# Unit 1's loads on GpSimd's queue, first-layer weights in three pieces, and landing delays in the planner

## The chip, the cores and the metric

The kernel runs on one core of a Trainium2 chip. The metric is device time in microseconds of one execution, lower is better. Engines are named as in the profile: PE (TensorE's matmuls; PEld its weight loads), DVE (VectorE), ACT (ScalarE), POOL (GpSimd) and SP (SyncE, which here only issues transfers).

## The reference

A gated linear recurrence is followed by a two-layer network with a squared ReLU. Per batch and head, a 48x48 state is decayed by alpha, receives the outer product of k and v, and is read by q; the outputs of the eight heads of a token, side by side, are the network's 384 inputs.

```python
batch, n_heads, seq, head_dim = (4, 8, 768, 48)
for t in range(S):
    state = alpha[:, :, t, :, None] * state + np.einsum('bhd,bhe->bhde', k[:, :, t], v[:, :, t])
    y[:, :, t] = np.einsum('bhd,bhde->bhe', q[:, :, t], state)
...
n_tokens, d_model, d_ff = (3072, 384, 2048)
h = x @ w_in
r = np.maximum(h, 0.0)
g = r * r
return (g @ w_out).astype(np.float32)
```

## The kernel before

The 3072 tokens are cut into twelve units of 256 tokens: unit g holds tokens of batch g % 4, and units 0 to 3 are the first third of each sequence. Each unit goes through a front (decays from alpha's logarithms, scaled keys and queries, transposes), scores with a causal mask, a state update, an output, then the first dense layer (eight groups of six matmuls, s1, each for two of the sixteen 128-column tiles of the hidden layer), ReLU and square, and the second dense layer (s2: two halves of the tokens, each in four parts of four matmuls over the hidden tiles).

Nothing is emitted in the order in which it is written. Every step is handed to `add` with its engine (or several to choose from), an estimated cost, a priority and what it reads and writes. `Program.schedule` then plays a list scheduler on those costs, in which transfers are modelled as three queues (SP, ACT, Pool) that share the bandwidth. It fixes each engine's order; `place` works out which semaphores each step must wait for, and `emit` writes the instructions. An engine works through its list strictly in order. Two tables correct the plan by hand: MOVED adds to a step's priority (larger is later) and CHOSEN fixes a step's engine. `fill` puts matmuls of zeros on the PE (line 1103) where the plan has it idle before the first s1 step.

The order of transfers is set by the queue that a transfer is issued on, by its priority there, and by AFTER, which makes an issue wait until another transfer has landed. `load(g)` issues alpha, k, q and v of a unit (384 KB each, tile raw, line 524). In the kernel before, SP issues the loads of all units but 2, and Pool those of unit 2 (POOL_LOADS) and the weights. `weight(lay, w)` issues each layer's weights in WS = 2 halves (tiles win and wout, line 495), read as float32 and written as bfloat16. AFTER reads there:

```python
AFTER = {(1, "v"): (0, "q"), ("win", 0): (1, "a"), ("win", 1): (1, "a"), 2: ("win", 0), ("wout", 0): ("win", 1),
         ("wout", 1): (2, "k"), 3: ("wout", 0)}
```

so both halves of the first layer wait for unit 1's alpha, unit 2's loads for the first half, the second layer's first half for the second half of the first layer, and unit 3's loads for the second layer's first half.

Lines that the prediction names: 524 a load's issue, 495 a weight's issue, 540 the logarithm of unit 0's alpha (ACT), 569 the cast of unit 0's v, 775 the state update, 904 scores, 915 the masks, 836 and 843 the output of the early units, 950 and 962 the transposes of a unit's activations and their copy to the tile xt, 1008 s1, 1016 and 1018 ReLU, 1026 and 1030 the square (sq, into the tile gt), 1049 s2, 879 the state's product with a decay (sbd).

Of the kernel before, what the change touches and what calls it, by code (L numbers as in the profile page):

```python
# [33 lines left out]
class Program:  # L34
# [9 lines left out]
    DMA_LAST = 800  # L44
    SWITCH = 95
# [67 lines left out]
    def schedule(self):  # L113
# [237 lines left out]
def bass_gla_recurrent__then__act_relu_squared_kernel(  # L351
# [13 lines left out]
    T = 256  # L365
    NST = S // T
    KT = DM // 128
# [12 lines left out]
    WS = 2  # L380
# [99 lines left out]
    FS = FT // WS  # L480

    def hidden(fj):

        w, e = divmod(fj, FS)
        return slice(w * FS * 128 + e, (w + 1) * FS * 128, FS)

    def weight(lay, w):
        cut = slice(w * FS * 128, (w + 1) * FS * 128) if lay == 0 else slice(w * FS, (w + 1) * FS)
        if lay == 0:
            src, dst = moe_w_in.rearrange("(kk p) n -> p kk n", p=128)[:, :, cut], WIN[:, :, cut]  # L490
        else:
            src = moe_w_out[w * FS * 128:(w + 1) * FS * 128, :].rearrange("(p e) n -> p (e n)", e=FS)
            dst = WOUT[:, cut, :].rearrange("p e n -> p (e n)")
        key = ("win", "wout")[lay]
        load_op[key, w] = add("pool", lambda e: e.dma_start(dst, src), 930, W_PRIO[lay] + w, writes=[(key, w)], name=f"{key}{w}",
                              dma=f"{key}{w}", lag=8600 / WS,
                              after=[load_op[AFTER[key, w]]] if (key, w) in AFTER else [])
# [3 lines left out]
    def hd(ap):  # L501
        return ap.rearrange("p (h d) -> p h d", h=H)

    def named(x):
        return next(o for o in pr.ops if o.name == x)
# [3 lines left out]
    def load(g):  # L509
        b, i = units[g]  # L510
        t0 = i * T
        p0 = g * P
        r, la, qs, kt, pm, vb, x2 = (g % n for n in (NRAW, 2, NQKS, NKQT, NPM, NV, 2))
        first, last = i == 0, i == NST - 1
        sr, sw = 2 * b + i % 2, 2 * b + (i + 1) % 2

        for j, t, nm in ((0, alpha, "a"), (1, k, "k"), (2, q, "q"), (3, v, "v")):
            src = t[b, :, t0:t0 + T, :].rearrange("h (p j) d -> p h (j d)", j=2)
            dst, key = RAW[r][:, j], ("raw", r, j)
            ring, cost, gate = "sp", 600, AFTER.get((g, nm), AFTER.get(g))  # L520
# [3 lines left out]
            load_op[g, nm] = add(ring, lambda e, dst=dst, src=src: e.dma_start(dst, src), cost, (L_PRIO[g] + j if ring == "sp" else W_PRIO[2] + 10 * g + j),  # L524
                writes=[key], name=f"ld{nm}{g}", dma=f"{nm}{r}{ring}", lag=1230,
                after=([load_op[gate]] if gate else []) + ([named(f"{BEHIND[nm]}{g - 1}")] if g >= 5 else []))
# [441 lines left out]
    def last_tile(gt, rows, p0):  # L968

        for h, cut in enumerate((slice(0, LAST_CUT), slice(LAST_CUT, DM))):  # L970
# [3 lines left out]
            def s2(pe, psS=psS, cut=cut):  # L974
# [5 lines left out]
                + [("wout", w) for w in range(WS)], writes=[keyS], name=f"s2_{G - 1}_1_{h}")  # L980
# [6 lines left out]
    def first_layer(g):  # L987
# [5 lines left out]
        for u in range(nb):  # L993
# [19 lines left out]
            add("pe", s1, pe_ns(KT * per, T), pu, reads=[("xt", s)] + sorted({("win", f // FS) for f in fjs}),  # L1013
# [18 lines left out]
    def second_layer(g):  # L1032
# [4 lines left out]
        for j in range(2):  # L1037
# [6 lines left out]
            for sg in range(4):  # L1044
                ps_ = p0 + P * 0.5 + 600 + (j * 4 + sg) * P * 0.5 / 8

                def s2(pe, sg=sg, j=j, psS=psS):
# [6 lines left out]
                    reads=[("gt", gt, fj) for fj in range(sg * FT // 4, (sg + 1) * FT // 4)] + [("wout", sg * WS // 4)],  # L1054
# [15 lines left out]
    W_PRIO = (-5e5, -4e5, -4.5e5)  # L1070
# [6 lines left out]
    AFTER.update({g: (g - 1, "q") for g in range(4, G)})  # L1077
    load(0)
    load(1)
    for w in range(WS):  # L1080
        weight(0, w)
    load(2)
    for w in range(WS):
        weight(1, w)
# [50 lines left out]
```

## Time and profile before

| | before |
|---|---|
| median of 3 runs | 176.35 us (176.1 to 176.62) |
| the profiled execution | 176.55 us, of which its span is 174.8 us |
| granted TensorE clock | 1.00 of full speed |
| PE busy | 168.1 us, 96% of the span, filler of 9.5 us included |
| DVE, ACT, POOL busy | 123.6, 113.9, 20.6 us |
| read from and written to HBM | 25.17 MB, 4.72 MB |
| transfers | 191 GB/s as a mean; Pool's queue 4.72 MB, SP's 28.32 MB |

Times in the views count from the span's start. A row of the timeline gives start, duration, engine, line, operation, output <- input, and in brackets the engine's idle time before it and what ended it. A row of a table by stretches gives the stretch, its length, busy time and number of instructions of each engine asked for, the granted clock, the share of the 16 DMA engines' time that packets took (over 1 when packets overlap in an engine) and GB/s. A row of issues gives the issuing queue, size and the time from issue to landing.

### The profile page before, as it was taken

Reading aid. Unit: us, or ns where it says so; the run is one execution under the profiler, and the core shown is the slowest. Engines: PE = TensorE matmul, PEld = TensorE weight load, DVE = VectorE, ACT = ScalarE, POOL = GpSimd, SP = SyncE. Lnnn points to the kernel's source line nnn. Section 1 sums busy time; section 2 is a strip of 40 time slices with the busy share of each in tenths; the row PEclk is TensorE's granted clock in tenths of the full one; section 3 lists DMA queues with packets and bytes.
Section 4 is the critical chain, followed back from the end, with each engine's and each line's share of the span. In section 5 each row is a group of like instructions: output and inputs, shape, how many; then the busy total and the mean of one; then the engine's idle time right before and its main releaser. Section 6 shows DMA issues by size and latency. Waiting matters only on the chain.

```text
span 174.8 us, 5089 instructions
## 1 busy us (share of the span) xinstructions
PE 168.1 (96%) x2233; PEld 130.7 (75%) x2235; DVE 123.6 (71%) x201; ACT 113.9 (65%) x205; POOL 20.6 (12%) x30
## 2 busy tenths in 40 slices
PE   7989799999999999999999999999999999999994
PEld 2655689765788588878778778788678797788773
DVE  5499597989879889988958858859659726322230
ACT  3745479637778677858688669588568564566440
POOL 3141561020402302100100100000000000000000
DMA  5999899999999899798997998899599691040022
GB/s 138 323 296 197 160 334 217 219 274 257 301 210 204 210 252 181 203 222 173 280 188 213 240 196 226 208 209 256 132 182 250 140 196 24 0 135 4 9 81 90
DMA packets 74742, 33.36 MB, mean 191 GB/s; under 512 B 71648, under 2 KB 71904, under 8 KB 74720
## 3 DMA queue, kind: packets, MB, share of 16 engines
q1 hardware_dynamic: 73184, 28.32, 70.8%
q0 software_dynamic: 1536, 4.72, 12.4%
q8 instruction: 17, 0.28, 0.6%
q14 instruction: 5, 0.04, 0.1%
HBM read 25.17 MB, written 4.72 MB: 171 GB/s over the span
## 4 chain that ended last, share of the span: by engine, by line
PE 78%; DMA 14%; ACT 3%; SPq 2%; issue 1%; DVE 0%
PE psWH L1008 33%; PE psO L1049 30%; DMA win<-in_moe_w_in_dram 5%; DMA raw<-in_alpha_dram 5%; DMA raw<-in_q_dram 3%; SPq L524 2%; PE psX L807 2%; PE psX L904 2%; PE psZ L775 2%; PE psWH L1049 2%; PE psX L976 2%; PE psX L796 1%; PE psZ L904 1%; ACT rr L1016 1%; PE psWH L648 1%; PE psO L1008 1%
## 5 line engine op out<-in xcount | busy, mean ns | idle before, releaser
L1008 PE MATMUL psWH<-xt,win 128*128 128x256 bf16 x552 | 70.8, 274 | 1.3 <-DMA win<-in_moe_w_in_dram 0.9
L1008 PEld LDWEIGHTS psWH<-xt,win 128*128 128x128 bf16 x552 | 62.8, 145 | 6.0 <-ACT rr L1016 1.2
L1049 PE MATMUL psO<-wout,gt 128*128 128x384 bf16 x352 | 66.5, 326 | 0.2 <-ACT osb L1056 0.2
L1016 ACT ACTIVATE rr<-psWH 128x512 bf16<-128x512 f32 x78 | 46.1, 595 | 21.2 <-PE psWH L1008 20.0
L1049 PEld LDWEIGHTS psO<-wout,gt 128*128 128x128 bf16 x352 | 33.0, 98 | 18.1 <-ACT osb L1056 0.4
L1026 DVE TENSOR_TENSOR gt<-rr 128x1024 bf16<-128x1024 bf16 (+1 forms) x45 | 27.2, 607 | 22.4 <-ACT rr L1016 22.0
L915 DVE TENSOR_TENSOR pm<-psX,caus 128x1024 bf16<-128x1024 f32 x12 | 14.6, 1219 | 0.9 <-PE psZ L904 0.9
L915 DVE TENSOR_TENSOR pm<-psZ,caus 128x1024 bf16<-128x1024 f32 x12 | 14.6, 1216 | 0.9 <-PE psZ L904 0.9
L1056 ACT ACTIVATE osb<-psO 128x384 f32<-128x384 f32 x18 | 8.8, 490 | 8.5 <-PE psO L1049 8.2
L1030 ACT ACTIVATE gt<-rr 128x1024 bf16<-128x1024 bf16 (+1 forms) x15 | 12.8, 857 | 1.8 <-DVE rr L1018 1.4
L710 DVE TENSOR_TENSOR qks<-raw,eq 128x384 bf16<-128x384 f32 x18 | 9.4, 554 | 4.1 <-DMA raw<-in_q_dram 3.9
L935 ACT ACTIVATE xbf<-psX 128x768 bf16<-128x768 f32 x10 | 8.1, 809 | 4.7 <-PE psX L796 4.4
L1018 DVE TENSOR_SCALAR rr<-psWH 128x512 bf16<-128x512 f32 x14 | 9.6, 686 | 1.9 <-PE psWH L1008 1.7
L1103 PE MATMUL psO<-zero 128*128 128x512 bf16 (+1 forms) x33 | 9.5, 422 | 1.4 <-DVE zero L445 1.3
L715 DVE TENSOR_TENSOR qks<-raw,ek 128x768 bf16<-128x768 f32 x11 | 10.7, 975 | 0.0
L706 ACT ACTIVATE vbf<-raw 128x768 bf16<-128x768 f32 x7 | 5.9, 839 | 4.1 <-DMA raw<-in_v_dram 4.1
L681 ACT ACTIVATE la<-raw 128x384 f32<-128x384 f32 x8 | 4.2, 521 | 4.8 <-DMA raw<-in_alpha_dram 4.7
L1103 PEld LDWEIGHTS psO<-zero 128*128 128x128 bf16 x35 | 3.5, 109 | 4.9 <-issue 1.9
L705 POOL CAST vbf<-raw 128x768 bf16<-128x768 f32 x4 | 3.5, 869 | 30.1 <-DMA raw<-in_v_dram 30.1
L870 DVE TENSOR_TENSOR smd<-psZ,sbd 128x384 bf16<-128x384 f32 x8 | 4.4, 555 | 3.6 <-PE psX L796 3.6
L640 ACT ACTIVATE lab<-prd 128x384 bf16<-128x384 f32 x10 | 5.2, 519 | 2.6 <-POOL prd L639 1.8
L879 POOL TENSOR_TENSOR sbd<-tmp,acm 128x384 bf16<-128x384 f32 x5 | 5.2, 1037 | 13.7 <-DVE tmp L877 13.7
(129 smaller groups left out, 180.7 us busy)
## 6 DMA issues: line engine op xcount, KB each, us to landing
raw<-in_alpha_dram SPq DMA_DIRECT2D x11, 384.0 KB, 3.8
raw<-in_k_dram SPq DMA_DIRECT2D x11, 384.0 KB, 4.8
raw<-in_q_dram SPq DMA_DIRECT2D x11, 384.0 KB, 4.2
raw<-in_v_dram SPq DMA_DIRECT2D x11, 384.0 KB, 4.9
out_dram<-osb SPq DMA_DIRECT2D x11, 384.0 KB, 4.0
win<-in_moe_w_in_dram POOLq DMA_DIRECT2D x2, 768.0 KB, 11.0
wout<-in_moe_w_out_dram POOLq DMA_DIRECT2D x2, 768.0 KB, 8.8
raw<-in_alpha_dram POOLq DMA_DIRECT2D x1, 384.0 KB, 4.6
```

Of the source, the lines that this page charges most:

```text
L710: add("dve", lambda e, j=j, dst=dst: e.tensor_tensor(dst, RAW[r][:, 2, :, j, :].rearrange("p (n x) d -> p n x d", x=2), EQ[la][:, j].rearr ...
L715: add("dve", lambda e, a=a, E=E: e.tensor_tensor(QKS[qs][:, a, :, :, 0:D], RAW[r][:, 1 + a].rearrange("p h j d -> p j h d"), E[la][:].rear ...
L915: add("dve", lambda e, hf=hf, psT=psT: e.tensor_tensor(PM[pm][:, hf].rearrange("p r n j t -> p (r n) (j t)"), psT[:, :, :].rearrange("p r ...
L935: add("act", lambda e: e.activation(XBF[x2][:], psX[:, :, 0:HD], AF.Copy), act_ns(2 * HD), p0 + 6100, reads=[("ps", "X", 0), ("ps", "X", 1 ...
L1008: ins = pe.matmul(psF[:, i * T:(i + 1) * T], WIN[:, kk, hidden(fj)], mov, start=(kk == 0), stop=(kk == KT - 1))
L1016: add("act", lambda e, psF=psF, rr=rr: e.activation(rr, psF, AF.Relu), act_ns(512), pu + 600, reads=[keyF], writes=[("rr", rb, half)], nam ...
L1018: alts={"dve": (lambda e, psF=psF, rr=rr: e.tensor_scalar(rr, psF, 0.0, None, ALU.max), dve_ns(512))})
L1026: add("dve", lambda e, dst=dst, sq=sq: e.tensor_tensor(dst, sq, sq, ALU.mult), 148 + k * 267, pu + 1200, reads=[("rr", rb, h) for h in ran ...
L1030: "act": (lambda e, dst=dst, sq=sq: e.activation(dst, sq, AF.Square), act_ns(k * 512))})
L1049: ins = pe.matmul(psS, GT[gt][:, fj, j, :], WOUT[:, fj, :], start=(fj == 0), stop=(fj == FT - 1))
L1056: add("act", lambda e, j=j, psS=psS: e.activation(OSB[ob][:, j], psS, AF.Copy), act_ns(DM), ps_ + 700, reads=[keyS], writes=[("osb", ob, j ...
L1103: pr.fill(lambda n: lambda pe: pe.matmul(psO[:, 0:n], ZERO[:, 0:128], ZERO[:, 0:n], skip_group_check=True), ((512, 216, 420), (256, 109, 2 ...
```

## The change

Unit 1's four loads leave SP's queue and go to Pool's, where one list, QUEUE, now sets the order: unit 1's loads, the first layer in three pieces of 4, 4 and 8 tiles (CUT), unit 2's loads, and the second layer in two. AFTER is rewritten: unit 1's alpha and k, and the first piece, wait for unit 0's alpha; its q and v, and the second piece, for unit 0's k; the third piece for unit 0's q; unit 2's loads for the second piece; the second layer's first half for the third piece and its second half for unit 2's k; unit 3's loads, as before, for the second layer's first half. The hidden layer's columns are dealt to tiles within a piece (`hidden`), and the second layer's rows are loaded to match. The planner's model of a transfer gets a delay by name (LATE), and MOVED and CHOSEN are new lists.

```diff
+    LATE = {"ld0": 300, "ld1": 450, "ld2": 800, "win0": 1000, "win1": 600, "win2": 600, "wout0": 800, "wout1": 500}
...
     MOVED = {
-       "s2_2_1_3": 7106, "y2": 20605, "vc2": 1344, "sq3_1": 11423, "re2_7": -11717, "re1_6": 4811, "sq3_5": -1032,
...
+       "s2_2_1_3": 39407, "s2_2_0_2": 34013, "s2_2_0_0": -42665, "lb5": 16519, "s1_2_6": 19412, "m1i5": -22795,
+        "s2_1_1_1": 168415, "sq0_7": 73172, "s2_2_1_2": 37834, "s1_0_5": 52602, "s2_0_1_3": 98172,
...
     CHOSEN = {
-       "re1_6": "dve", "et1_2": "act", "sq2_3": "act", "bk4": "pool", "xv3": "act", "re3_2": "dve", "sq3_5": "dve",
+       "et10_0": "dve", "vc1": "pool", "et0_1": "act", "sq0_7": "act", "sd1": "pool", "re1_1": "dve", "sq1_5": "act",
+        "et1_2": "act", "oe0_1": "act", "sa3": "dve", "sq2_1": "pool", "sq2_3": "act", "re2_5": "dve",
+        "sq2_6": "act", "sq2_7": "pool", "sd4": "pool", "re3_3": "act", "sq3_3": "dve", "re3_5": "dve",
+        "sq3_6": "pool", "sq3_7": "pool", "sq4_1": "dve", "pr6": "pool", "vc6": "pool",
     }
...
-                    land(op, t + self.DMA_LAST)
+                    unit = "ld" + op.name[3:] if op.name.startswith("ld") else op.name
+                    land(op, t + self.DMA_LAST + self.LATE.get(unit, 0))
...
-    POOL_LOADS = {2: "akqv"}
+    CUT = (4, 4, 8)
+    QUEUE = "a1 k1 q1 v1 win0 win1 win2 a2 k2 q2 v2 wout0 wout1".split()
...
+    def piece(fj):
+
+        w, w0 = 0, 0
+        while fj >= w0 + CUT[w]:
+            w, w0 = w + 1, w0 + CUT[w]
+        return w, w0, CUT[w]
...
-        w, e = divmod(fj, FS)
-        return slice(w * FS * 128 + e, (w + 1) * FS * 128, FS)
...
+        w, w0, n = piece(fj)
+        return slice(w0 * 128 + fj - w0, (w0 + n) * 128, n)
...
+    def weight(name):
+        key, w = name[:-1], int(name[-1])
+        if key == "win":
+            w0, n = sum(CUT[:w]), CUT[w]
+            cut = slice(w0 * 128, (w0 + n) * 128)
             src, dst = moe_w_in.rearrange("(kk p) n -> p kk n", p=128)[:, :, cut], WIN[:, :, cut]
         else:
...
+            w0, n, e = 8 * w, 8, piece(8 * w)[2]
+            src = moe_w_out[w0 * 128:(w0 + n) * 128, :].rearrange("(s p e) n -> p s (e n)", p=128, e=e)
+            dst = WOUT[:, w0:w0 + n, :].rearrange("p (s e) n -> p s (e n)", e=e)
+        load_op[name] = add("pool", lambda e: e.dma_start(dst, src), 930, -6e5 + QUEUE.index(name), writes=[(key, w)], name=name,
+                            dma=name, lag=8600 * n / 16, after=gate(name))
...
-            if nm in POOL_LOADS.get(g, ""):
-                ring, cost = "pool", 930
...
+            if name in QUEUE:
+                ring, cost, at = "pool", 930, -6e5 + QUEUE.index(name)
...
-    AFTER = {(1, "v"): (0, "q"), ("win", 0): (1, "a"), ("win", 1): (1, "a"), 2: ("win", 0), ("wout", 0): ("win", 1),
-             ("wout", 1): (2, "k"), 3: ("wout", 0)}
+    AFTER = {"win0": "a0", "a1": "a0", "k1": "a0", "q1": "k0", "v1": "k0", "win1": "k0", "win2": "q0", "a2": "win1", "k2": "win1",
+             "q2": "win1", "v2": "win1", "wout0": "win2", "wout1": "k2", 3: "wout0"}
```

More of the change, by code (lines that the diff above doesn't have):

```diff
@@ L376, in bass_gla_recurrent__then__act_relu_squared_kernel @@
     DENSE = {0: 19172, 1: 35978, 2: 46351, 3: 61182, 11: 160500}
-    POOL_LOADS = {2: "akqv"}
+    CUT = (4, 4, 8)
+    QUEUE = "a1 k1 q1 v1 win0 win1 win2 a2 k2 q2 v2 wout0 wout1".split()
     RATIO = 4
     NRAW, NQKS, NKQT, NPM, NV, NXT, NGT, NRR, NOSB = 4, 3, 3, 2, 4, 4, 2, 4, 2
-    WS = 2
     LATE_STATE = (1, 2)
@@ L502, in hd, with gate @@
         return ap.rearrange("p (h d) -> p h d", h=H)
+    def gate(*names):
+        return [load_op[AFTER[x]] for x in names if x in AFTER][:1]
     def named(x):
@@ L979, in last_tile @@
             add("pe", s2, pe_ns(FT, n), p0 + h, reads=[("gt", gt, fj) for fj in range(FT)]
-                + [("wout", w) for w in range(WS)], writes=[keyS], name=f"s2_{G - 1}_1_{h}")
+                + [("wout", w) for w in range(2)], writes=[keyS], name=f"s2_{G - 1}_1_{h}")
             add("act", lambda e, psS=psS, cut=cut: e.activation(OSL[:, cut], psS, AF.Copy), act_ns(n), p0 + 700 + h,
@@ L1012, in first_layer @@
             fjs = range(u * per, (u + 1) * per)
-            add("pe", s1, pe_ns(KT * per, T), pu, reads=[("xt", s)] + sorted({("win", f // FS) for f in fjs}),
+            add("pe", s1, pe_ns(KT * per, T), pu, reads=[("xt", s)] + sorted({("win", piece(f)[0]) for f in fjs}),
                 writes=[keyF], name=f"s1_{g}_{u}")
@@ L1053, in second_layer @@
                 add("pe", s2, pe_ns(FT // 4, DM), ps_,
-                    reads=[("gt", gt, fj) for fj in range(sg * FT // 4, (sg + 1) * FT // 4)] + [("wout", sg * WS // 4)],
+                    reads=[("gt", gt, fj) for fj in range(sg * FT // 4, (sg + 1) * FT // 4)] + [("wout", sg // 2)],
                     writes=[keyS], name=f"s2_{g}_{j}_{sg}")
@@ L1069, in bass_gla_recurrent__then__act_relu_squared_kernel @@
     L_PRIO[0], L_PRIO[1] = -9e5, -8e5
-    W_PRIO = (-5e5, -4e5, -4.5e5)
     ORDER = ["f0", "k0", "p0", "f1", "y0", "p1", "k1", "y1", "f2", "p2", "k2", "s0", "s1"]
@@ L1074, in bass_gla_recurrent__then__act_relu_squared_kernel @@
     ORDER += [f"y{G - 1}"]
-    AFTER = {(1, "v"): (0, "q"), ("win", 0): (1, "a"), ("win", 1): (1, "a"), 2: ("win", 0), ("wout", 0): ("win", 1),
-             ("wout", 1): (2, "k"), 3: ("wout", 0)}
-    AFTER.update({g: (g - 1, "q") for g in range(4, G)})
+    AFTER = {"win0": "a0", "a1": "a0", "k1": "a0", "q1": "k0", "v1": "k0", "win1": "k0", "win2": "q0", "a2": "win1", "k2": "win1",
+             "q2": "win1", "v2": "win1", "wout0": "win2", "wout1": "k2", 3: "wout0"}
+    AFTER.update({g: f"q{g - 1}" for g in range(4, G)})
     load(0)
[L1079 to L1084, printed above, removed]
+    early = []
+    for x in QUEUE:
+        if x[0] == "w":
+            weight(x)
+        elif int(x[1:]) not in early:
+            early.append(int(x[1:]))
+            load(early[-1])
+    for g in (1, 2):
+        if g not in early:
+            load(g)
     for st in ORDER:
```

19 lines of the change are left out of this document (5 added, 14 removed), and 7 rows, old and new, of the table MOVED.

## The prediction, made before the changed kernel ran

> **What bounds the kernel now.** I read the shares of the page first, then the busy time of TensorE in stretches that I cut where its work changes, then the chain of waits, and last the timeline and the DMA queues of the first 37 us.
>
> The page's first line, and TensorE alone by stretch (length, busy time and instructions, granted clock, DMA share, GB/s):
>
> ```profile
> PE 168.1 (96%) x2233; PEld 130.7 (75%) x2235; DVE 123.6 (71%) x201; ACT 113.9 (65%) x205; POOL 20.6 (12%) x30
> ...
> 16.78:19.03 2.25, 1.39 (x37) 1.00 1.14 214
> 19.03:23.50 4.47, 4.23 (x80) 1.00 0.82 213
> 23.50:32.20 8.70, 8.70 (x93) 1.00 1.04 247
> 32.20:37.00 4.80, 4.35 (x65) 1.00 1.05 261
> 37.00:172.55 135.55, 134.69 (x1788) 1.00 0.81 179
> ```
>
> From 19.03 us on, TensorE stands still for only 0.24 + 0.00 + 0.45 + 0.86 = 1.55 us, at full clock. No edit to loads can shorten that stretch by more; what is left to win lies ahead of 19.03, where the first dense group (six matmuls of line 1008) begins. What holds it back is in the chain and the timeline:
>
> ```profile
> 9.42 9.56 DMA win<-in_moe_w_in_dram
> 19.03 0.87 PE psWH L1008 x6
> ...
> 16.22 0.56 DVE L962 COPY xt<-psX 128x768 bf16<-128x768 bf16 x1
> 17.53 0.42 PE L904 MATMUL psX<-kqt 64*64 64x128 bf16 x16
> 17.77 0.39 PE L904 MATMUL psZ<-kqt 64*64 64x128 bf16 x16
> ```
>
> Unit 0's activations are ready at 16.22 + 0.56 = 16.78 us. Until 19.03 TensorE has only unit 1's scores (17.53 to 18.16, 0.63 us) and filler, and waits for the first half of the first-layer weights. So 2.25 - 0.63 = 1.62 us are lost there. With the 1.55 us above, 3.17 us is all that can be had while xt0 is ready at 16.78: a floor of 176.55 - 3.17 = 173.4 us against the profiled execution (176.55 us, of which 174.8 is span). That execution is 0.2 us above the median of the runs, 176.35.
>
> **What the first landing costs the rest.** The weights go through one queue, and they are limited by transfer:
>
> ```profile
> L495 POOL DMA_DIRECT2D win<-in_moe_w_in_dram x2: 788/860/932, 9.4 to 10.4; - x2
> DMA to landing us min/median/max: 9.6/11.0/12.4
> ...
> q1 hardware_dynamic: 864, 0.33, 117.5%
> ...
> q0 software_dynamic: 723, 1.44, 108.4%
> ...
> 23.51 0.88 PE L1008 MATMUL psO<-xt,win 128*128 128x256 bf16 x6
> 19.03:23.50 4.47, 3.06 (x24) 2.59 (x24) 1.00 0.82 213
> ```
>
> The first two lines are the tile win: issues at 9.4 and 10.4, landings at 9.4 + 9.6 = 19.0 and 10.4 + 12.4 = 22.8 us. The two queue lines are the transfers of 9 to 10 us (SP's loads) and of 12.7 to 20 us (Pool's weights): packets, MB, share of 16 engines' time. The engines are full in both, so landings go by the bytes queued ahead. A packet of a load takes 1.175 x 16 / 864 = 21.8 ns for 384 bytes, one of the weights 1.084 x 7.3 x 16 / 723 = 175 ns for 2 KB in SBUF (4 KB of float32 read). The last line is line 1008 alone: 24 matmuls, four of unit 0's eight groups, are done by 23.50. The fifth, the first to need the second half, starts at 23.51, 0.7 us after that half landed.
>
> **The change, part by part.**
>
> *Unit 1's loads to Pool.* SP loses four issues, and Pool gains four. Unit 1's alpha and k now wait for unit 0's alpha, q and v for unit 0's k.
>
> ```profile
> 4.35 0.94 ACT L540 ACTIVATE laf<-raw 128x384 bf16<-128x384 f32 x2 [0.96 <-DMA raw<-in_alpha_dram]
> 3.09 1.15 SPq L524 DMA_DIRECT2D raw<-in_v_dram  x1
> raw<-in_v_dram SPq DMA_DIRECT2D x1, 384.0 KB, 4.8
> 19.27 0.95 POOL L524 DMA_DIRECT2D raw<-in_alpha_dram  x1 [5.71 <-DMA win<-in_moe_w_in_dram]
> 20.21 0.89 POOL L524 DMA_DIRECT2D raw<-in_k_dram  x1
> 7.97 0.82 POOL L569 CAST vbf<-raw 128x768 bf16<-128x768 f32 x1 [5.03 <-DMA raw<-in_v_dram]
> 13.89 0.36 PE L836 MATMUL psX<-smd,kqt 128*64 128x96 bf16 x8
> ```
>
> Unit 0's alpha has landed by 4.35, its v lands at 3.09 + 4.8 = 7.9. Pool then issues at 4.3, 5.3, 6.2 and 7.1 (0.95 and 0.89 us each), and the three first-layer pieces at about 8.0, 8.8 and 9.7 by the 0.86 us above, done at 10.5. SP's queue works until 7.9, and two Pool loads are issued by then. So the DMA engines find work without a gap, and unit 1's loads pass as they did. Cost: nothing, covered by unit 0's transfers; without that cover it would be Pool's lead from issue to first byte, under 2 us (19.27 to where the queue is full again at 21.0, below). What queues behind these issues on Pool is unit 0's v cast (7.97 before): it goes to ACT or waits until 10.5, done by 11.4. Unit 0's output reads it at 13.89. Cost 0, at most 0.5.
>
> *Pieces of 4, 4 and 8 tiles.* The first piece is half as long. Ahead of it lie eight loads, and the weights' data began right behind the last of these before too. It should land about 393 KB earlier at the 1.44 MB in 7.3 us above: 2.0 us before 19.0, at 17.0; if some engines lag, as the late landings suggest, 16 to 17.5. Unit 0's first two groups thus start at about 17.0, its next two need the second piece near 19.0. Half-size packets: a line through 21.8 ns for 384 bytes and 175 ns for 4 KB gives 90 ns for 2 KB, so two cost 181 where one cost 175. For 384 packets' worth on 16 engines that is 24 x 6 ns, about 0.15 us later for the last piece. If a packet cost 175 ns whatever its size, it would be 24 x 175 ns = 4.2 us. The loads' small packets show time going with bytes, so I take 0.15 and keep a little of the other end in the range.
>
> So the last piece lands at 22.8 + 0.15 = 22.9 or 23.0. This limits the gain: groups five to eight still wait for it. By then TensorE has done four groups, unit 1's scores, state and output. Before, it was there at 23.51, so 0.55 us are won, and 0.35 more if unit 1's x-transposes (0.34 us at 25.04) are done by then too, since unit 1's output no longer stands behind late groups:
>
> ```profile
> 19.36 1.21 DVE L915 TENSOR_TENSOR pm<-psX,caus 128x1024 bf16<-128x1024 f32 x1
> 22.78 0.29 PE psX L836 x8
> 25.04 0.34 PE psX L950 x6
> ```
>
> Unit 1's last mask ends at 20.57 and its output ran at 22.78; it may run near 21.2, and its transposes, 2.3 us behind it before with two groups between, near 23.
>
> *Unit 2's loads and the second layer.* They wait for the second piece instead of the first half, the second layer's first half for the last piece.
>
> ```profile
> 23.00 0.56 POOL L495 DMA_DIRECT2D wout<-in_moe_w_out_dram  x1
> wout<-in_moe_w_out_dram POOLq DMA_DIRECT2D x1, 768.0 KB, 7.8
> 32.20 1.46 PE L1049 MATMUL psO<-wout,gt 128*128 128x384 bf16 x8
> ...
> q0 software_dynamic: 9, 0.02, 28.6%
> ```
>
> The second layer's first half landed at 30.8, and was first used at 32.20. The last line is 20.4 to 21.0 us: the engines ran nearly empty there, since unit 2's loads were issued at 19.27. Issued behind the second piece, while the last is still moving, they close that gap, 0.4 us, which pays for the 0.15. So weights needed at 32.2 - 0.9 = 31.3 are there by about 30.6, and this wait is hidden by 0.7 us. If that cover went, the gain would.
>
> *The planner.* Due times and engine choices of some 40 steps change. They add no work for TensorE. A better order may recover a part of the 0.45 us of 32.20 to 37.00; I take 0.2 (bounds: plus 1.55, and a loss that the second rival prices).
>
> Sum: 0.55 + 0.35 + 0.2 = 1.1 us. 176.55 - 1.1 = 175.45 against the profiled execution, 175.25 against the median: 175.3. The forecast's own range is 0.6 to 2.0 us of gain, 174.4 to 175.8, because the last piece may land up to a microsecond sooner (a single late engine may have set 22.8).
>
> **The rivals.**
>
> *Nothing comes of it.* The last piece is no earlier than the second half was, so groups start earlier and TensorE waits longer before the fifth. For this: the engines are full from 9 to 20 us and no byte is removed. Against: unit 1's output moves ahead. If the last piece lands at 23.4 or later, within 0.5 us of before: 176.3.
>
> *Squares on Pool (slower).* The new table puts unit 2's and 3's squares sq2_1 (1024 columns), sq2_7, sq3_6 and sq3_7 (512) on Pool, which now has none.
>
> ```profile
> 22.18 0.68 DVE L1026 TENSOR_TENSOR gt<-rr 128x1024 bf16<-128x1024 bf16 x1
> 23.45 1.53 DVE L1026 TENSOR_TENSOR gt<-rr 128x1024 bf16<-128x1024 bf16 x1
> 23.57 0.85 POOL L879 TENSOR_TENSOR sbd<-tmp,acm 128x384 bf16<-128x384 f32 x1
> L879 POOL TENSOR_TENSOR sbd<-tmp,acm 128x384 bf16<-128x384 f32 x5 | 5.2, 1037 | 13.7 <-DVE tmp L877 13.7
> L1026 DVE TENSOR_TENSOR gt<-rr 128x512 bf16<-128x512 bf16 x17 | 7.2, 423 | 3.9 <-ACT rr L1016 3.8
> ```
>
> Pool takes 1.04 us for 384 columns, so 1.4 us for 512 against VectorE's 0.42, and 2.8 for 1024. Beside Pool's 0.85 us the same VectorE square took 1.53 instead of 0.68: it waited Pool out. The last squares of a unit release the last quarter of its second layer. If TensorE waits for three of them at 1.4 - 0.4 = 1.0 us, and VectorE is held for 2 us at the other, up to 3 to 4 us are lost; with the gain of 1.1, about +2: 178.3. It decides once a square ends after TensorE has run out of other groups. Against: TensorE holds two units' groups at a time.
>
> *Queues that take turns (slower).* If SP's and Pool's queues shared an engine packet by packet, unit 0's v would starve.
>
> ```profile
> DMA packets 201, 0.70 MB, mean 350 GB/s; under 512 B 29, under 2 KB 29, under 8 KB 201
> 30.85 0.37 SPq L524 DMA_DIRECT2D raw<-in_alpha_dram  x1
> q0 software_dynamic: 67, 0.41, 97.5%
> q1 hardware_dynamic: 1, 0.00, 0.1%
> ```
>
> Pool's loads (22 to 24 us) move in 172 packets of 4.1 KB, 0.19 us each. From about 6.2 to 7.9 us SP has some 1.7 / 0.0218 = 78 packets per engine left; a Pool packet before each makes 78 x 0.21 = 16 us, v lands near 22 and the first group starts near 26: about 183 us. [...] SP's load was issued at 30.85, and from 31.5 to 33.6 us Pool's queue moved 67 packets and SP's one. The queue that was at work stayed at work, and here that is SP's.
>
> **How the numbers follow.** Forecast 0.50; nothing comes of it 0.22; squares or another step of the new order 0.22; turns 0.06. About 0.3%, 0.5 us, is what a measurement of this kernel tells from no change. Faster by more 0.50, within it 0.22, slower 0.28. The range runs from 173.8 (most of the floor) to 177.8 (the squares' rival, three quarters of it): left out are the turns, 0.06, the worst of the squares, 0.07, and 0.05 below.
>
> **What would show it.** Right: unit 1's four loads on Pool; the first group of line 1008 at 16.8 to 17.5 instead of 19.03; the fifth at 22.5 to 23.2; line 1049 beginning at 31 to 31.7; TensorE still under 2.5 us idle from there. Wrong: a wait of line 1008 for win beyond 23.4; unit 0's v after 9 us; line 1049 waiting for VectorE's or Pool's gt between 45 and 70 us; a first group before 16.

## The result, and the profile after

The changed kernel takes 175.27 us (median of 20 runs, 174.0 to 178.15), the kernel before, run beside it, 176.25 us (20 runs). The ratio is 0.993, 95% interval 0.9907 to 0.9952: a gain of 1.0 us. Some executions of either kernel are disturbed and take up to 5% longer: medians here include them, ratios leave them out, and since the first profile of the changed kernel (178.15 us) fell into one, the profile shown is of the same kernel run again: 175.45 us, span 173.7 us. Against the profiled execution of before (176.55 us, 174.8 us) that is 1.1 us. Line numbers moved: s1 is now line 1023, s2 1064, scores 919, masks 930, unit 1's output 851, the copy to xt 977.

First the page's line of TensorE, then TensorE by stretches, cut where its work changes (length, busy time and instructions, granted clock, DMA share, GB/s), both after the change:

```profile
PE 167.4 (96%) x2235; PEld 129.3 (74%) x2235; DVE 118.1 (68%) x192; ACT 119.1 (69%) x212; POOL 29.1 (17%) x37
```

```profile
17.04:22.83 5.79, 4.74 (x112) 1.00 1.05 272
22.83:31.30 8.47, 8.47 (x95) 1.00 1.07 235
31.30:37.00 5.70, 5.70 (x81) 1.00 1.04 263
37.00:171.50 134.50, 133.00 (x1773) 1.00 0.80 178
```

The starts of the same steps, from the timeline of TensorE after:

```profile
17.04 1.50 PE L1023 MATMUL psWH<-xt,win 128*128 128x256 bf16 x12
18.47 0.42 PE L919 MATMUL psX<-kqt 64*64 64x128 bf16 x16
...
22.04 0.36 PE L851 MATMUL psX<-smd,kqt 128*64 128x96 bf16 x8 [1.05 <-DVE smd L888]
...
22.84 1.53 PE L1023 MATMUL psWH<-xt,win 128*128 128x256 bf16 x12
...
31.19 1.46 PE L1064 MATMUL psO<-wout,gt 128*128 128x384 bf16 x8
```

| step | before | after | lead |
|---|---|---|---|
| first dense group | 19.03 | 17.04 | 1.99 |
| fifth dense group | 23.51 | 22.84 | 0.67 |
| second layer begins | 32.20 | 31.19 | 1.01 |
| span | 174.8 | 173.7 | 1.1 |

Read the table from the top: 2.0 us are won at the first group, two thirds of that are lost again by the fifth, and 1.1 us arrive at the end. The stretches show the loss: from the first dense group on, TensorE idles 1.05 + 0 + 0 + 1.50 = 2.55 us, where it idled 1.55 before. So 1.0 of the 2.0 us went back into idle time. The 1.05 us are one wait, for smd, in front of unit 1's output. The third row of the table isn't quite like for like: from the fifth group's start on, ten groups have run by 31.19 us after the change, and eleven by 32.20 us before it, with eight transposes fewer.

Who TensorE waits for, after (the view of waits: total us, times, longest; one wait of 1.3 us at the very start is left out), the first-layer weights, and the chain of waits around the early groups:

```profile
PE psX L851 <- DVE smd L888: 1.0, 1, 1.0
PE psX L811 <- DVE pm L930: 0.8, 1, 0.8
PE psX L919 <- DMA kqt<-qks: 0.4, 1, 0.4
```

```profile
L507 POOL DMA_DIRECT2D win<-in_moe_w_in_dram x3: 760/767/782, 8.3 to 9.8; - x3
...
DMA to landing us min/median/max: 6.5/8.3/11.3
```

```profile
16.42 0.57 DVE xt L977
...
18.54 0.35 PE psX L919 x16
...
19.16 2.35 DVE pm L930 x2
21.52 0.48 DVE smd L888
```

The wait for win, 0.9 us in the kernel before, is gone from the list. The first piece landed at 8.3 + 6.5 = 14.8 us, the last at 9.8 + 11.3 = 21.1. What releases the first group is now unit 0's own front: xt is ready at 16.42 + 0.57 = 16.99 us, and the group starts at 17.04.

### The profile page after: what moved, and what is told of

It is laid out like the page before. It is cut to its first block, busy times and chain, and to the rows that moved or that the text cites. A ratio compares the mean times of both kernels' runs of the same rounds, so it can differ in the third digit from the quotient of the medians.

```text
span 176.4 us, 5099 instructions
## 1 busy us (share of the span) xinstructions
PE 168.9 (96%) x2235; PEld 129.8 (74%) x2235; DVE 118.7 (67%) x192; ACT 119.6 (68%) x212; POOL 29.6 (17%) x37
## 3 DMA queue, kind: packets, MB, share of 16 engines
q0 software_dynamic: 2512, 6.29, 15.2%
## 4 chain that ended last, share of the span: by engine, by line
PE 78%; DMA 11%; DVE 7%; ACT 1%; SPq 1%; issue 1%; DVEq 0%
PE psWH L1023 30%; PE psO L1064 26%; DMA raw<-in_q_dram 6%; PE psO L1121 5%; DMA raw<-in_alpha_dram 3%; DVE pm L930 3%; DMA kqt<-qks 2%; PE psX L919 2%; PE psX L822 2%; PE psZ L790 2%; PE psX L991 2%; PE psX L811 1%; PE psZ L919 1%; PE psWH L1064 1%; PE psX L858 1%; PE psZ L753 1%
## 5 line engine op out<-in xcount | busy, mean ns | idle before, releaser
L1023 PEld LDWEIGHTS psWH<-xt,win 128*128 128x128 bf16 x552 | 61.5, 130 | 6.3 <-DVE xt L977 0.7
L1031 ACT ACTIVATE rr<-psWH 128x512 bf16<-128x512 f32 x79 | 46.9, 596 | 18.8 <-PE psWH L1023 17.4
L1064 PEld LDWEIGHTS psO<-wout,gt 128*128 128x128 bf16 x352 | 33.5, 98 | 18.0 <-issue 0.5
L1041 DVE TENSOR_TENSOR gt<-rr 128x1024 bf16<-128x1024 bf16 (+1 forms) x38 | 22.9, 606 | 22.9 <-ACT rr L1031 22.7
L1045 ACT ACTIVATE gt<-rr 128x1024 bf16<-128x1024 bf16 (+1 forms) x18 | 14.9, 840 | 1.5 <-DVE rr L1033 1.0
L950 ACT ACTIVATE xbf<-psX 128x768 bf16<-128x768 f32 x11 | 8.9, 810 | 8.1 <-PE psX L811 6.2
L720 POOL CAST vbf<-raw 128x768 bf16<-128x768 f32 x5 | 4.9, 974 | 29.5 <-DMA raw<-in_v_dram 29.5
L1044 POOL TENSOR_TENSOR gt<-rr 128x512 bf16<-128x512 bf16 (+1 forms) x4 | 5.4, 1348 | 26.2 <-ACT rr L1031 24.2
L652 DVE TENSOR_TENSOR prd<-raw 128x384 f32<-128x384 f32 x8 | 4.8, 600 | 3.2 <-DMA raw<-in_alpha_dram 3.2
L683 DVE TENSOR_TENSOR ek<-ek,raw 128x384 f32<-128x384 f32 x10 | 5.9, 589 | 1.5 <-ACT ek L674 1.5
```

Of the source, the lines that this page charges most:

```text
L950: add("act", lambda e: e.activation(XBF[x2][:], psX[:, :, 0:HD], AF.Copy), act_ns(2 * HD), p0 + 6100, reads=[("ps", "X", 0), ("ps", "X", 1 ...
L1023: ins = pe.matmul(psF[:, i * T:(i + 1) * T], WIN[:, kk, hidden(fj)], mov, start=(kk == 0), stop=(kk == KT - 1))
L1031: add("act", lambda e, psF=psF, rr=rr: e.activation(rr, psF, AF.Relu), act_ns(512), pu + 600, reads=[keyF], writes=[("rr", rb, half)], nam ...
L1041: add("dve", lambda e, dst=dst, sq=sq: e.tensor_tensor(dst, sq, sq, ALU.mult), 148 + k * 267, pu + 1200, reads=[("rr", rb, h) for h in ran ...
L1045: "act": (lambda e, dst=dst, sq=sq: e.activation(dst, sq, AF.Square), act_ns(k * 512))})
L1064: ins = pe.matmul(psS, GT[gt][:, fj, j, :], WOUT[:, fj, :], start=(fj == 0), stop=(fj == FT - 1))
```

## The experiments

Three sets of runs, each beside its own runs of the kernel before, which had medians of 178.07, 177.65 and 176.84 us. Runs of one kernel spread by 1 to 5%, so a difference under 1 us is read from the interval of the ratio and from the profile together.

**The changed kernel again**, with no edit.

> The changed kernel again, as the yardstick for the runs beside it, with a profile at full clock. Both theories: 1.0 us under the kernel before (ratio 0.993 to 0.995); first group of the first layer at 16.7 us, its fifth at 22.5, second layer from 31.0; TensorE idle under 3 us after 16.75.

Median 176.3 us against 178.07; the ratio is 1.0017, interval 0.9952 to 1.0081. This set can't tell the gain from nothing; its profile, shown above, is the evidence for where the time went.

**The new order alone**: the transfers of before, with the new tables and the delays.

```diff
 # the kernel before, with
+    LATE = {...}        # as in the change
     MOVED, CHOSEN       # the new lists
```

> The transfers of before with the new priorities, engine choices and landing delays. Theory A (the transfers make the gain, the planner's part is 0.2 us): within 0.4 us of before, 176.0 to 176.6, because the first group still waits for the first half of the weights until 19.0. Theory B (the new order makes the gain): 175.2 to 175.6.

177.32 us, ratio 0.9994 (0.994 to 1.0047), profiled span 173.9 us. The interval holds both no change and a gain of half a per cent, so the order alone shows no gain that this set can measure. Its one profile is as short as the changed kernel's; its weights landed early for the old transfers (first group at 17.87 us), as told below.

**The new transfers alone**: queue, pieces and gates of the change, the old tables, no delays.

```diff
 # the changed kernel, with
-    LATE = {"ld0": 300, ...}
+    LATE = {}
     MOVED, CHOSEN       # the lists of before
```

> Unit 1's loads on Pool and the weights in 4, 4 and 8 tiles, with the old priorities and engine choices and no landing delays. Theory A: 0.6 to 1.1 us under before, 175.1 to 175.7, first group at 16.7 to 17. Theory B: no gain, 176.2 or more, because TensorE stops later for the old order's steps.

181.7 us, ratio 1.0272 (1.0188 to 1.0356): 2.7% slower. TensorE by stretches, and the first of its waits:

```profile
31.00:60.00 29.00, 27.02 (x378) 1.00 1.01 235
60.00:120.00 60.00, 57.13 (x829) 1.00 0.90 195
```

```profile
PE psX L962 <- ACT xbf L947: 1.2, 2, 0.9
PE psWH L1020 <- ACT xt L976: 0.9, 1, 0.9
```

TensorE idles 1.98 us from 31 to 60 and 2.87 from 60 to 120, mostly waiting for results of ScalarE and VectorE, not for weights. The two tables are corrections to one particular plan; with other transfers, and here without the delays too, the same corrections give another order, and it is a worse one. So the parts can't be added up: transfers and tables belong together. The next runs therefore hold the order fixed. They take the changed kernel with its planned engine and start of every step written into a table, and edit one thing; where only transfers are edited, TensorE's 2235 matmuls run in the changed kernel's sequence. Their s1 is line 1688 or 1689, s2 1729 and unit 1's output 1516 or 1517.

**The transfers, at one order**: the order of the change, the transfers of before.

```diff
-    CUT = (4, 4, 8)
+    CUT = (8, 8)
-            if name in QUEUE:
+            if name in QUEUE and g != 1:
-    AFTER = {"win0": "a0", "a1": "a0", ...}
+    AFTER = {"v1": "q0", "win0": "a1", "win1": "a1", "a2": "win0", ..., "wout0": "win1", "wout1": "k2", 3: "wout0"}
```

> The changed kernel's order on every compute engine with the transfers of before: unit 1's loads on SP, the first layer in two halves that wait for unit 1's alpha, unit 2's loads behind the first half. Theory A (at one and the same order the earlier landing of the first layer is the gain): first group at 18 to 19 instead of 16.7 to 17.0, second layer from 32.2 or later, and 1 to 2 us slower than changed, so level with before or up to 1 us slower. Theory B (the new order is the gain): within 0.4 us of the changed kernel.

177.75 us, ratio 1.0001 (0.9956 to 1.0045). The tile win and TensorE's timeline:

```profile
L1172 POOL DMA_DIRECT2D win<-in_moe_w_in_dram x2: 786/864/943, 9.4 to 10.3; - x2
...
DMA to landing us min/median/max: 9.7/11.1/12.5
```

```profile
19.21 1.50 PE L1688 MATMUL psWH<-xt,win 128*128 128x256 bf16 x12 [2.06 <-DMA win<-in_moe_w_in_dram]
...
33.61 1.47 PE L1729 MATMUL psO<-wout,gt 128*128 128x384 bf16 x8
```

The old wait is back, 2.06 us long, and the halves land at 19.1 and 22.8 as before. The first group is 2.2 us later than in the changed kernel, the second layer 2.4, and the profiled span is 176.3 us against 173.7: the 2.2 us stay lost to the end. With the order held, the profile puts the gain in the transfers, and the ratio agrees: no gain without them. This ratio and the gain's 0.993 come from different sets, though, and the changed kernel's own repeat gave 1.0017, so part of the gain could lie elsewhere.

**Halves instead of pieces**, unit 1's loads still on Pool.

```diff
-    CUT = (4, 4, 8)
+    CUT = (8, 8)
-    QUEUE = "a1 k1 q1 v1 win0 win1 win2 a2 ...
+    QUEUE = "a1 k1 q1 v1 win0 win1 a2 ...
```

> The changed kernel with every compute engine's order held as it was, and the first layer in two pieces of 8 tiles again; unit 2's loads wait for the first of them. Theory A (the start of the first group carries to the end one to one): first 8 tiles land near 17.2, the first group starts there instead of 16.75 to 17.0, and the second layer starts 0.2 to 0.4 us later. Theory B (the masks behind unit 1's scores set the fifth group): the scores stand behind two groups, so it is the same 0.2 to 0.4. A result over 1 us slower would say that pieces matter for more than the first landing.

177.16 us, ratio 0.9954 (0.991 to 0.9999), span 175.8 us. Its tile win, and TensorE's timeline:

```profile
L1172 POOL DMA_DIRECT2D win<-in_moe_w_in_dram x2: 767/774/782, 8.3 to 9.0; - x2
...
DMA to landing us min/median/max: 8.7/10.2/11.7
```

```profile
17.11 1.50 PE L1688 MATMUL psWH<-xt,win 128*128 128x256 bf16 x12 [0.73 <-DVE kqt L1425]
...
31.36 1.46 PE L1729 MATMUL psO<-wout,gt 128*128 128x384 bf16 x8
```

The halves land at 17.0 and 20.7 us, and the first group starts at 17.11, the second layer at 31.36: within 0.2 us of the changed kernel. Moving unit 1's loads to Pool, with the earlier issue that follows from it, brings the weights 2 us forward without the pieces; most of these 2 us are one late signal of sixteen, as told below. In these profiles the cut into pieces is worth little to these two starts, since the front is ready no sooner. The span is 2.1 us longer than the changed kernel's all the same, and that is lost late: TensorE's steps are 0.2 us behind at the second layer's start, 0.5 at 88 us and 2.0 at the last step (170.62 against 168.60 us). I know no reason for it in the edit. Executions of the changed kernel's repeat at full clock have spans from 172.6 to 175.0 us, so a single profile can differ by that much, and a lead at the start needn't show at its end.

**Unit 1's loads on SP again**, pieces and gates as in the change, so the weight pieces are issued at 4.7 to 7.1 us on Pool while SP's loads still move.

```diff
-            if name in QUEUE:
+            if name in QUEUE and g != 1:
```

> The changed kernel with every compute engine's order held as it was, and only unit 1's four loads back on SP's queue, so that Pool issues the three weight pieces from 4.5 us on, while SP still has loads to move. Theory A (an engine stays with the queue that it works on): the pieces begin when SP's last load is through, near 12.6; unit 1's loads land at 9 to 13 as before, the first piece at 15 to 17, and the end is within 0.5 us of the changed kernel's. Theory B (queues take turns by packet): the weights' larger packets crowd out SP's, unit 0's v lands after 10 and unit 1's v after 17, the first group starts over 1 us later, and the kernel is 1 us or more slower than changed.

182.86 us, ratio 1.0244 (1.0179 to 1.0309). The DMA queues from 10 to 13 us; unit 1's alpha (issued at 4.43); two of TensorE's steps; and TensorE by stretches:

```profile
q0 software_dynamic: 454, 0.45, 88.7%
q1 hardware_dynamic: 445, 0.17, 31.4%
```

```profile
raw<-in_alpha_dram SPq DMA_DIRECT2D x1, 384.0 KB, 9.7
```

```profile
15.12 0.48 PE L1293 MATMUL psWH<-laf,linc 128*128 128x384 bf16 x1 [3.85 <-ACT laf L1289]
...
23.17 1.50 PE L1689 MATMUL psWH<-xt,win 128*128 128x256 bf16 x12
```

```profile
10.00:12.00 2.00, 1.27 (x38) 1.00 1.20 205
12.00:14.00 2.00, 0.00 (x0) 0.80 1.20 210
14.00:16.00 2.00, 0.88 (x3) 0.50 1.12 211
16.00:18.00 2.00, 2.00 (x28) 0.50 1.12 216
18.00:20.00 2.00, 2.00 (x6) 0.50 1.14 305
20.00:21.00 1.00, 1.00 (x42) 0.98 1.04 280
```

Here both queues have work on the same engines, and they take turns: 454 packets of the one, 445 of the other. A load's packet holds 0.17 MB / 445 = 382 bytes, a weight's 0.45 MB / 454 = 0.99 KB, so turns by packet give the loads the small share of the bytes. Unit 0's v, nearly through when Pool's first data move at 7.75 us, still lands at 8.1. Unit 1's alpha lands at 4.43 + 9.7 = 14.1 us, TensorE stands still for 3.85 us, its clock falls to half, and the first group starts 6.1 us later than in the changed kernel.

**Pool's first two loads earlier**: unit 1's alpha and k no longer wait for unit 0's alpha, and are issued from 2.89 us on instead of 4.54. It was run once.

```diff
-    AFTER = {"win0": "a0", "a1": "a0", "k1": "a0", "q1": "k0", ...
+    AFTER = {"win0": "a0", "q1": "k0", ...
```

> The changed kernel with orders held, and unit 1's alpha and k issued by Pool at about 3 us, without their wait for unit 0's alpha, while SP's loads of unit 0 are under way. Theory A (an engine stays with the queue that it works on until that runs empty): unit 0's v still lands at 7.9 and unit 1's alpha at 9.1. Theory B (turns by packet): unit 0's k, q or v land late, v after 12. Theory C (first come, first served over both queues): v after one or two Pool loads, at 9 to 10.3, and unit 1's alpha ahead of it, at 7 to 8.5.

178.31 us, span 176.6 us. The queues from 6.25 to 7 us and from 8.25 to 9 us, when Pool's first and second load move beside unit 0's v (issued at 3.01); that load's landing; TensorE by stretches; and the first group:

```profile
q0 software_dynamic: 67, 0.28, 97.5%
q1 hardware_dynamic: 36, 0.01, 6.4%
...
q0 software_dynamic: 55, 0.23, 93.5%
q1 hardware_dynamic: 82, 0.03, 16.2%
```

```profile
raw<-in_v_dram SPq DMA_DIRECT2D x1, 384.0 KB, 7.5
```

```profile
10.00:12.00 2.00, 0.61 (x16) 0.76 1.00 306
12.00:14.00 2.00, 2.00 (x30) 0.50 1.24 206
```

```profile
19.83 1.50 PE L1689 MATMUL psWH<-xt,win 128*128 128x256 bf16 x12
```

Unit 0's v lands at 3.01 + 7.5 = 10.5 us instead of 8.1, TensorE waits 2.48 us for what is made from it, until 11.39, its clock falls to half, and the first group is 2.8 us late. Pool's packets hold 0.28 MB / 67 = 4.2 KB here, eleven rows of 384 bytes, SP's a row each. In the two stretches together the queues move 122 and 118 packets, and 0.51 and 0.04 MB: about a packet for a packet again, whatever it holds, though not in each stretch by itself. Turns of single rows or of equal bytes would have given SP about half of the bytes. Between them, from 7.25 to 8 us, Pool moves only 7 packets and SP runs nearly alone, so v loses about two loads' time and not more. None of the three theories has this whole: v is late as in B but lands before 12 us, and the landings, 8.1 us for unit 1's alpha and 10.5 for v, are near those of C.

**The four squares on VectorE** instead of Pool, the order otherwise held.

```diff
-    "sq2_1#0": ("pool", ...   # and sq2_7, sq3_6, sq3_7
+    "sq2_1#0": ("dve", ...
```

> The changed kernel with orders held, and the four squares of units 2 and 3 that Pool does moved to VectorE at the same places. Theory A (Pool's squares are hidden): within 0.3 us of the changed kernel. Theory B (they cost TensorE waits of a microsecond each, as the second rival of the prediction had it): 1 to 3 us faster than the changed kernel.

177.4 us, ratio 0.9972 (0.9926 to 1.0017), span 174.8 us: no faster than the changed kernel by its profile (173.7 us), and no gain that the interval can show. The Pool squares in the changed kernel's trace:

```profile
L1044 POOL TENSOR_TENSOR gt<-rr x4: 1038/1228/1893, 48.1 to 69.6; 128x512 bf16<-128x512 bf16 x3, 128x1024 bf16<-128x1024 bf16 x1
```

The view of who waited for them is empty.

**The fifth group ahead of unit 1's output.**

```diff
-    "s1_0_4#0": ("pe", 23265.06, ...
+    "s1_0_4#0": ("pe", 21750.06, ...   # just before y1
```

> The changed kernel with orders held but for one step: unit 0's fifth group goes ahead of unit 1's output on TensorE, into the 1.05 us in which TensorE waited for the masked state. Theory A (that wait is all lost time): the wait shrinks to 0.4 us, the second layer starts 0.65 us sooner, and the kernel is 0.4 to 0.65 us faster than changed. Theory B (the last piece lands too late to fill it, or the time is given back later): no gain, or up to 0.5 us slower, with a wait of line 1023 for win.

175.19 us, ratio 0.9944 (0.9903 to 0.9985); the changed kernel's own ratio is 0.993, so no gain on top of it is seen. TensorE's timeline:

```profile
21.43 0.85 PE L1689 MATMUL psWH<-xt,win 128*128 128x256 bf16 x6 [1.09 <-DMA win<-in_moe_w_in_dram]
22.21 0.36 PE L1517 MATMUL psX<-smd,kqt 128*64 128x96 bf16 x8
```

The wait of 1.05 us for smd becomes a wait of 1.09 for the last piece, which landed at 21.3 here. The two limits lie that close.

**No delays in the planner**, everything else as in the change.

```diff
-    LATE = {"ld0": 300, ...}
+    LATE = {}
```

> The changed kernel without the landing delays in the planner; priorities and choices as changed. Theory A: within 0.3 us of the changed kernel, since the delays only move where the planner puts steps. Theory B: over 0.5 us slower than the changed kernel, since the tables were drawn up with the delays and TensorE's order then meets transfers that are not there.

176.93 us, ratio 0.9947 (0.9889 to 1.0006), span 173.8 us. This plan too puts the fifth group before unit 1's output:

```profile
21.80 1.50 PE L1023 MATMUL psWH<-xt,win 128*128 128x256 bf16 x12 [1.21 <-DMA win<-in_moe_w_in_dram]
```

TensorE then waits 1.21 us for the weights instead of 1.05 for smd, and the time can't be told from the changed kernel's.

**Two newly drawn-up orders**, to look for a faster version: other tables, the first with the change's delays, the second with delays nearer to the landings measured. The transfers and gates are the change's, but the tables also swap some neighbours on the queues.

```diff
     MOVED, CHOSEN       # drawn up anew for each
-    LATE = {"ld0": 300, "ld1": 450, "ld2": 800, "win0": 1000, "win1": 600, "win2": 600, "wout0": 800, "wout1": 500}
+    LATE = {"ld0": 300, "ld1": 300, "ld2": 500, "win0": 300, "win1": 500, "win2": 300, "wout0": 500, "wout1": 100}   # the second only
```

> The changed kernel with a longer search over the planner's two tables (the delays as changed; the first two weight pieces and unit 0's q and v change places on their queues). Theory A (TensorE's remaining waits after the first group, 2.4 us, are a matter of order): under 1.5 us of waits left and 0.5 to 1 us faster than changed. Theory B (they move with the landings of each run, so an order fitted closer to one set of delays gains nothing): within 0.4 us of changed or slower.

> The same search with the delays set nearer to the landings that the changed kernel's profile shows (first piece 0.3 instead of 1.0, last 0.3 instead of 0.6 and so on). Theory A (truer delays make a better order): as fast as the searched order or up to 0.3 us faster, with the first group at 16.7 to 17.7. Theory B: waits for transfers that come later than planned, and no gain over changed.

The first takes 176.28 us, ratio 0.9949 (0.9909 to 0.999), the second 178.17, ratio 1.0048 (1.0002 to 1.0093). The first is level with the changed kernel. The second, with truer delays, is slower, its first group starting at 18.45 us; as its loads come in another order too, that isn't shown to be the delays' doing. No version that was run is clearly faster than the changed kernel.

## Why the prediction was right, and where its reasons weren't

**The sum.** Forecast 0.55 + 0.35 + 0.2 = 1.1 us; measured 1.1 between the profiled executions and 1.0 between the medians. The size is right, the terms less so.

**First term, the fifth group (0.55 forecast, 0.67 measured, for another reason).** The step that failed is the landing of the weights. I put the first piece at 17.0 us and the last at 22.9; they landed at 14.8 and 21.1. My argument was that landings go by the bytes queued ahead. A transfer's landing is 16 signals in the trace, and the landings above (19.0 and 22.8 us before, 14.8 and 21.1 after) are the last of each sixteen. Worked out from these records (us, 15 signals from first to last, then the sixteenth; to about 0.1 us):

```
the kernel before            first half    16.4 to 17.2    19.0
                             second half   20.1 to 20.9    22.7
transfers of before, held    first half    16.3 to 17.1    19.1
                             second half   20.0 to 20.8    22.8
the new order alone          first half    16.5 to 17.8    17.8
                             second half   20.2 to 21.5    21.6
halves instead of pieces     first half    15.8 to 16.9    17.0
                             second half   19.4 to 20.6    20.7
the changed kernel           last piece    19.7 to 20.6    21.1
no delays in the planner     last piece    19.6 to 20.4    21.7
```

In the profile of before that I forecast from, one signal comes 1.8 to 1.9 us after the other fifteen and alone sets the landing. The same happens with the transfers of before at the held order; in the run of the new order alone, with the same transfers, the last signal is 0.1 us or less behind the next. With unit 1's loads on Pool it is 0.1 us behind in the run of halves, 0.5 in the changed kernel and 1.2 without delays (20.43 and 21.67), under the same transfers as the changed kernel's. So fifteen signals fit landings that go by the bytes, and differ by half a microsecond or less between halves with unit 1's loads on SP and on Pool; the late signal belongs to the execution as much as to the transfers. Taking 1.8 and 1.9 us off my two numbers gives 17.0 - 1.8 = 15.2 and 22.9 - 1.9 = 21.0, close to the 14.8 and 21.1 measured. The prediction named a single late engine, only as a reason for the width of its range; which engine a signal belongs to, the trace doesn't say. Why the signal lags is open. A fetch of instructions (a packet of 16 KB in the page's queue q8 instruction, 0.88 to 1.24 us each in the trace of before) is a candidate that no run tested. One comes ahead of the lag, at 15.6 us before and at 16.8 with the old transfers held; the new order alone has it at 11.9, and there unit 1's v has a signal 1.4 us late. But with one at 14.2 in the run of halves no signal is late. A small part of the rest is rate: before, SP's loads alone, from 9 to 12 us, and after, Pool's queue alone, from 8 to 11.5 us:

```profile
DMA packets 2557, 0.97 MB, mean 323 GB/s; under 512 B 2557, under 2 KB 2557, under 8 KB 2557
```

```profile
q0 software_dynamic: 335, 1.18, 104.2%
```

The first is 323 GB/s, the second 1.18 MB in 3.5 us, about 336 GB/s. Four loads of 393 KB take 4.9 us at the one and 4.7 at the other, 0.2 us.

So I had the last piece as what the fifth group waits for, and it had been there for 1.7 us. What came late instead is unit 1's output, which I moved ahead to 21.2 us. I followed it to its mask's old end, 20.57, but not what stands in front of that mask. TensorE runs its list in the planned order, and in the new order unit 1's scores stand behind the first two dense groups: they start at 18.47 instead of 17.53. VectorE's two masks then run from 19.16 to 21.52, smd follows until 21.99, and the output runs at 22.04, with the fifth group behind it. The landing that I took for the limit would have let the fifth group go at 21.4 us, as the run with that group ahead shows (21.43, waiting for win). Weights 1.8 us sooner and an output 0.8 us later than I had them nearly cancelled, and that the number came out is luck.

**Second term, unit 1's transposes and the second layer (0.35).** The transposes did not run by 22.84; they start at 24.2, after two more groups. The second layer begins 1.01 us early, 0.9 by my first two terms, but with one group fewer done, as said above. That weights for it are there in time held: TensorE doesn't wait for wout in the first stretches, which have no idle time from 22.83 to 37.00.

**Third term, the planner (0.2 forecast, about -0.2 measured).** Before, TensorE idled 0.45 us from 32.20 to 37.00 and 0.86 after it, 1.31 in all. Now it is 0 and 1.50: the first was won, as I took it could be, and 0.64 given back later, in waits such as those for a mask (0.8, at 88 us) and for a transposed tile (0.4) shown above. The kernel before has no such wait for a mask. In the held order it is 0.6 us with the old transfers, 1.1 with halves and 1.5 with the squares on VectorE, so it varies by about the size of the gain.

**What the terms leave open.** The start is 1.99 us earlier, idle time costs 1.00 of that, and unit 1's scores (0.63), ahead of the first group before, now come behind it. That leaves 0.36, where the last matmul ends about 1.05 earlier (172.55 against 171.50). The gap is in the busy time from the first group on: 4.74 + 8.47 + 5.70 + 133.00 = 151.91 us after, 4.23 + 8.70 + 4.35 + 134.69 = 151.97 before, equal though the scores came in. So the other matmuls, the same by count to within three, took 0.7 us less together. Why they ran closer I don't know, and one profile of each can't say whether it would repeat.

**The rival "nothing comes of it".** It was to decide at a landing of the last piece at 23.4 or later. It landed at 21.1. With the transfers of before under the new order (last half at 22.8) the ratio is 1.0001: that is the time the rival would have given.

**The rival "squares on Pool".** The price per square was too high, 1.04, 1.04 and 1.42 us for 512 columns against my 1.4, and 1.89 for 1024 against 2.8. What decides is that nobody waited, and taking the squares off Pool made nothing faster. The reason that I gave against the rival, that TensorE holds two units' groups at a time, fits this and wasn't tested.

**The rival "turns".** It didn't decide, as I said, but my reason was wrong. I argued from the row of 31.5 to 33.6 us that a queue at work stays at work. The same trace at the end of that row, 33.5 to 34 us:

```profile
q0 software_dynamic: 16, 0.04, 40.3%
q1 hardware_dynamic: 116, 0.04, 34.2%
```

SP's load, issued at 30.85, has its first data at 33.56, 2.7 us after its issue, just as Pool's queue thins out (16 packets in this half microsecond). So the row can't say whether a turn was refused: it may be precedence, or the time until this load's first data while Pool's packets kept the engines busy (97.5%). With nothing else moving, SP's first load took 1.1 us (0.80 to 1.93); beside SP's working queue Pool's first data came 2.6 us after the issue in the changed kernel, 3.0 and 3.1 in the two runs that overlap the queues. I read one row as a rule. Those two runs show the turns once both queues have data, and what they cost: 6.1 and 2.8 us at the first group. The counts, 454 to 445 and 122 to 118, are about a packet for a packet, as this rival supposes, and the row that I set against it was no ground for a chance of 0.06.

What protects the changed kernel is timing. Its queues from 4.5 to 7.3 us:

```profile
q1 hardware_dynamic: 2334, 0.88, 113.7%
q0 software_dynamic: 5, 0.02, 3.1%
```

Pool's first load is issued at 4.54, and by 7.3 us it has moved 5 packets. Its first data come 2.6 us after the issue, and by then SP's last load is nearly through: unit 0's v, issued at 3.07, landed 5.0 us later, at 8.1 against 7.9 before. I put the cover at no cost and didn't ask how thick it is. It is thin: issuing 1.65 us earlier cost 2.8 us at the first group.

## What to carry to other kernels

In the two runs where both queues had data for the same engines, these moved about a packet for a packet (454 to 445, 122 to 118), and the loads with the small packets came late: 382 bytes against 0.99 KB, and 384 bytes against 4.2 KB, with the first group 6.1 and 2.8 us later. So put loads and weights in one queue, in the order in which they are needed, or be sure that the second starts as the first ends. A hand-corrected order belongs to the transfers it was drawn up for: the new transfers under the old tables, and without the delays, lost 2.7%; with their own they gained 0.7%. And when a step moves ahead in an engine's list, follow what now stands behind it to its last user; here two dense groups moved ahead of the scores, and the masks, the state and the output moved back with them.

## What the runs showed of the hardware that I had not expected

The clock. In the run with unit 1's loads on SP, TensorE waits 3.85 us, from 11.27 to 15.12 us, and the granted clock is 0.80 over 12 to 14 us, 0.50 from 14 to 20, and 0.98 from 20 to 21, some 5 us after work came back. All six runs of that kernel show a mean clock below 1 (0.981 to 0.991). In the run with Pool's first loads earlier the wait is 2.48 us, from 8.91 to 11.39, and the clock is 0.76 over 10 to 12 us and 0.50 from 12 to 14. An estimate, if these two stretches hold only the levels 1.00 and 0.50 that the stretches beside them show: a mean of 0.80 or 0.76 over 2 us is full clock for 1.2 or 1.0 us and half after it, so it fell at about 13.2 and 11.0 us, some 2 us into the wait. In the kernels before and after the clock stays at 1.00 here, and their longest waits behind the first 1.3 us of the span are 0.9 and 1.05 us; with the transfers of before at the held order it stays at 1.00 through a wait of 2.06 us too. In the two runs the late load thus cost twice, the wait and the slow matmuls after it: the eight filler matmuls that take 1.69 us in the changed kernel, at a clock of 1.00, took 3.04 us from 17.26 on in the run with unit 1's loads on SP.
